# A tuned attention and two-layer MLP kernel: another order of work in the first chunks, and late tiles laid out later

## The chip, the core and the metric

The kernel runs on one core of one Trainium2 chip. The metric is the device time in microseconds of one execution. A core has a matrix engine (TensorE, PE), three engines for elementwise work (VectorE or DVE, ScalarE or ACT, GpSimd or POOL), and a queue engine (SyncE, SP) that issues most of the transfers here. Each engine works through its own list of instructions in order; semaphores between the lists hold an instruction back until what it needs is done.

## The reference

Three parts follow one another. First a gated linear attention over 4 batches, 8 heads, 768 positions, head dimension 48; then a SiLU layer; then a gated SiLU layer.

```python
for t in range(S):                                   # S = 768
    state = alpha[:, :, t, :, None] * state + einsum('bhd,bhe->bhde', k[:, :, t], v[:, :, t])
    y[:, :, t] = einsum('bhd,bhde->bhe', q[:, :, t], state)
x = y as (3072, 384)
h = x @ w_in;  x1 = silu(h) @ w_out                  # d_ff = 2048
out = (silu(x1 @ w_gate) * (x1 @ w_val)) @ w_out2    # d_ff = 1536
```

## The kernel before, in words

The attention is cut into chunks of 128 positions: 6 per batch, 24 in all, numbered so that chunk n belongs to batch n % 4. In a chunk the 8 heads lie in 4 pairs, and a "duo" d is two pairs, so chunk n has duos 2n and 2n + 1. For a chunk, VectorE makes two running products of alpha (scan_r with a reciprocal, scan_g); GpSimd multiplies keys and queries by them (kq, two instructions per chunk, line 443); TensorE makes the scores of each duo (scores2, 16 small matmuls, line 463); VectorE applies the causal mask and writes pt (mask2, line 474); ScalarE copies the scaled keys out (keys2, line 480); TensorE multiplies by the values and adds up the state (pv, lines 654 to 677); ScalarE and VectorE split the result into a high and a low part (chunk_high, chunk_end) as input x of the first layer, since the products are done in two float32r parts.

The first 7 chunks (NF = 7, blocks 0 and 1 of the token blocks) are done ahead of everything else by early(m), called for m = 0 to 6. early(m) makes the scores of chunk m and the products pv of chunk m - 1, and it prepares chunk m + 2 (scans and kq). In chunks 0 to 3 (NE = 4) the values of the first pair are also spread into a second tile v3 by GpSimd (spread, line 686). filler issues matmuls of the mask with itself into the part of the yd tile that nobody reads; they are called clock keepers in the change. The yd tile holds the results of pv; from m = 3 on it also serves, before pv writes it, as scratch space for decoding one unit of the first layer's weights (early_unit: three VectorE passes, lines 93, 98 and 103, and later a high and a low part). The loop over the 7 chunks is the whole opening of the kernel; after it the first layer runs turn by turn (g1, act1, g2 over steps), with the later chunks of attention and the remaining weight decoding threaded in, and then the second layer.

The order of work is written out by hand: each call above appends to the engines' lists, so the order of calls in early is the order in each engine's list. What SP issues is in such a list too: load_in(n) loads alpha, keys and queries of chunk n into one of two buffers and is called at the end of scan_g(n - 2); load_v(n) loads the values of chunk n, also into one of two buffers, and is called at the end of chunk_end(n - 2); load1 loads raw weight units, two per chunk. Of pt there are three buffers, each for one duo; of the score banks two, of the yd banks two.

open_late (line 346) lays out the tiles that the later chunks of attention use: GpSimd sets four of them to zero (line 351, 359) and ScalarE copies four identities (line 353). It stands between the opening and the first product's SiLU (act1, lines 840 and 841, with a VectorE subtract for the low part gl).

Of the kernel before, what the change touches and what calls it, by code (L numbers as in the profile page):

```python
# [23 lines left out]
NCH = B * NC  # L24
NP = H // 2
# [243 lines left out]
def fast(ctx, tc, pk, w1, w2, out, bad_i):  # L269
# [5 lines left out]
    blocks1, n = [], 0  # L275
# [91 lines left out]
    in_t, raw_in, v_t, r_t = {}, {}, {}, {}  # L367
# [35 lines left out]
            load_in(later_in.pop(0)[1])  # L403

    def load_v(n):
        if n >= NCH:
            return
        v_t[n] = ap.tile([128, NP, C], F32, tag="in_v", name=f"in_v{n}")
        SP.dma_start(
            out=v_t[n], in_=pk[n, :, A_W + 2 * W:].rearrange("p (r e) -> p r e", r=NP)  # L410
        )
# [6 lines left out]
    def scan_r(n, i, k):  # L418


        rg, cs = rg4[n % 2], slice(i * CA, (i + k) * CA)
        DVE.tensor_tensor_scan(
            out=rg[:, 0, cs][:, ::-1], data0=in_t[n][0][:, cs.start + 1:cs.stop + 1][:, ::-1],
            data1=ones4[:, i:i + k].rearrange("p i t -> p (i t)")[:, ::-1], initial=0.0,
            op0=ALU.mult, op1=ALU.add,
        )
        DVE.reciprocal(
            out=rc4[:, i:i + k, 0], in_=rg[:, 0].rearrange("p (i t) -> p i t", i=NP)[:, i:i + k, 0]
        )

    def scan_g(n, i, k):


        rg, cs = rg4[n % 2], slice(i * CA, (i + k) * CA)
        DVE.tensor_tensor_scan(
            out=rg[:, 1, cs], data0=in_t[n][0][:, cs],
            data1=rc4[:, i:i + k].rearrange("p i t -> p (i t)"), initial=0.0, op0=ALU.mult, op1=ALU.add,
        )
        by_pair = rg.rearrange("p x (i t) -> p x i t", i=NP)
        for lo in range(i, i + k, 2):  # L440
            d = (n * NP + lo) // 2
            kq_t[d] = kqs[d % 6]
            (DVE if d == 0 else POOL).tensor_tensor(
                out=kq_t[d][:, :, :2 * C].rearrange("p i (x t) -> p x i t", x=2),
                in0=in_t[n][1][:, :, lo:lo + 2], in1=by_pair[:, :, lo:lo + 2, 1:], op=ALU.mult,
            )
        c, b = divmod(n, B)
        if c:
            for p in range(i, i + k):
                t = state[b][:, p]  # L450
                ACT.activation(out=t, in_=t, func=AF.Copy, scale=by_pair[:, 0, p, 0:1])
        if i + k == NP:
            load_in(n + 2)
# [15 lines left out]
    def mask2(d, s):  # L469

        pt = ap.tile([128, 2, 2, C], F32, tag="pt", name=f"pt{d}", bufs=3)
        pt_t[2 * d], pt_t[2 * d + 1] = pt[:, 0], pt[:, 1]
        wide = mask.rearrange("p (a o t) -> p a o t", a=1, o=1).to_broadcast([128, 2, 2, C])
        DVE.tensor_tensor(out=pt, in0=s[:, :, :, :C], in1=wide, op=ALU.mult)
# [7 lines left out]
    def early(m):  # L482

        if m == 0:
            yd_place(0)
        s = {}
        for d in (2 * m, 2 * m + 1):
            filler(max(m - 1, 0), 4 if d == 1 else 1)  # L490
            s[d] = scores2(d)
        if m:
            pv(m - 1)
        for d in s:
            mask2(d, s[d])
            keys2(d, s[d])
            if m == 0:
                (scan_r if d == 0 else scan_g)(1, 0, NP)
        if m:
            chunk_high(m - 1)  # L500
            yd_place(m)
        if m < NE:
            spread(m)
        if m + 2 < NF:
            scan_r(m + 2, 0, NP)
            scan_g(m + 2, 0, NP)
        if m >= 3:
            early_unit(yd_t[m][:, 512:])
        if m:
            chunk_end(m - 1)  # L510
        up_to("gd", 2 * m, guard, ND)
        up_to("l1", 2 * m + 1, load1, NU1)
# [91 lines left out]
    def yd_place(n):  # L604

        t = yd_t[n] = banks((6, 2)[(NF - 1 - n) % 2] if n < NF else 6, f"yd{n}")
        y_t[n] = t[:, 256:768]

    def filler(n, times):

        wide = mask.rearrange("p (o t) -> p o t", o=1).to_broadcast([128, 4, C])
        for _ in range(times):
            PE.matmul(
                yd_t[n][:, :512].rearrange("p (o t) -> p o t", o=4), mask, wide, start=True, stop=True
            )
# [22 lines left out]
    def pv(n):  # L638

        c, b = divmod(n, B)
        v = v_t[n]
        if n >= NF:
            yd_place(n)
        y = y_t[n]
        first, last = n * NP, n * NP + NP
        heads = [(p, h, slice(64 * h, 64 * h + 64)) for p in range(NP) for h in range(2)]
        pts = [pt_t.pop(g) for g in range(first, last)]
        for p, h, hs in heads:  # L650
            if n < NE and p == 0:
                continue
            cs, r = slice(p * C, p * C + C), half(p, h)
            PE.matmul(  # L654
                y[r:r + 64, cs], v[:, p, hs], pts[p][:, h], start=p in (n < NE, 2), stop=True,
                skip_group_check=True,
            )
            if n < NE:
                PE.matmul(
                    y[r:r + 64, cs], v3[n % 2][:, p - 1, hs], pts[0][:, h], start=False, stop=True,  # L660
                    skip_group_check=True,
                )
        if c < NC - 1:
            ds = ds_t[n] = yd_t[n][:, 768:768 + NP * D].rearrange("p (r e) -> p r e", r=NP)
            for p, h, hs in heads:
                PE.matmul(
                    ds[hs, p], kt_t[first + p][:, hs], v[:, p, 64 * h:64 * h + D],
                    start=False, stop=True, skip_group_check=True,
                )
            for g in range(first, last):  # L670
                kt_t.pop(g)
        if c:
            for p, h, hs in (heads[2 * p + h] for p in (0, 2, 1, 3) for h in range(2)):
                r = half(p, h)
                PE.matmul(
                    y[r:r + D, p * C:p * C + C], state[b][hs, p],
                    kq_t[(first + p) // 2][(hs, p % 2, slice(C, 2 * C)) if n < NF else (hs, 1, p % 2)],
                    start=False, stop=True,
                    skip_group_check=True,
                )  # L680

    def spread(n):


        t = v3[n % 2].rearrange("p k (h x) -> p k h x", h=2)
        POOL.tensor_copy(
            t[:, :, :, D:],
            v_t[n][:, 0].rearrange("p (h x) -> p h x", h=2)[:, :, :D].rearrange(
                "p h (k r) -> p k h r", k=KT
            ),  # L690
        )

    def chunk_high(n):

        c, b = divmod(n, B)
        y = y_t[n].rearrange("p (r t) -> p r t", r=NP)
        j, i = chunk_blk[n]
        if i == 0:
            x_t[j] = big(block_place(j), f"x{j}", F32R).rearrange("p (x k t) -> p x k t", x=2, k=KT)
            if j:  # L700
                y3_t[j] = mp.tile([128, 2, 512], F32R, tag="y3", name=f"y3_{j}", bufs=1)
        cs = slice(i * C, i * C + C)
        if urgent(n):
            return
        ACT.activation(
            out=x_t[j][:, 0, :, cs], in_=y[:, 1:], func=AF.Copy, accum_out=ysum[:, 0, n:n + 1]
        )
# [127 lines left out]
    def act1(j, f):  # L835
        w = len(blocks1[j]) * C
        hb = h_t.pop((j, f))
        gh = mp.tile([128, 512], F32R, tag="gh", name=f"gh{j}_{f}")[:, :w]
        gl = mp.tile([128, 512], F32R, tag="gl", name=f"gl{j}_{f}")[:, :w]
        ACT.activation(out=gh, in_=hb, func=AF.Silu)  # L840
        ACT.activation(out=hb, in_=hb, func=AF.Silu)  # L841
        act_t[j, f] = (gh, gl)

        def rest():
            sub(DVE, gl, hb, gh)

        return rest
# [701 lines left out]
    attn(1, False)  # L1549
    up_to("gd", first_d - 1, guard, ND)  # L1550
    estack.close()
    open_late()
    g1(0)
    rest = act1(*steps[0])
    units1()
    rest()
    for s, (j, f) in enumerate(steps):
        need1(2 * f + 1)
        if s == 0:
            units1()  # L1560
        n = 19 + 2 * (s + 3 - len(steps))
        if s + 1 < len(steps):
            need1(2 * steps[s + 1][1])
            if n >= 19:
                run(OUTPUT[n] - PAIR)
            g1(s + 1)
        slot(s, 0, (lambda: act1(*steps[s + 1])) if s + 1 < len(steps) else None)
        if n >= 19:
            if s + 1 < len(steps):
                free_banks.append((s + 1) % 2)  # L1570
            run(OUTPUT[min(n + 1, 23)] - PAIR)
        g2(j, f)
        slot(s, 1)

    wstack.close()
    free_banks += [2, 3, 4]
# [90 lines left out]
```

## Time and profile before

| | |
|---|---|
| time, median of 3 runs | 947.0 us (943.33 to 947.2) |
| profiled execution | 947.71 us, span 946.0 us |
| TensorE busy | 905.8 us (96%) |
| VectorE busy | 611.6 us (65%) |
| ScalarE busy | 451.4 us (48%) |
| GpSimd busy | 279.4 us (30%) |
| mean granted clock of TensorE | 0.982 of full speed |
| moved by DMA | 150.89 MB, mean 160 GB/s |

The span runs from the first to the last instruction that the profiler records; the time of the execution is a little longer. Busy shares are means over stages that have different limits, so they don't say by themselves what bounds a stage. Idle time of an engine is put down to what released it. The granted clock is the share of TensorE's full speed that it was given.

### The profile page before, as it was taken

How to read it: one execution, taken by the hardware profiler on the slowest of the kernel's cores; microseconds unless marked ns; L12 is line 12 of the kernel's file. 1: busy time of each engine (PE TensorE's matmuls, PEld its weight loads, DVE VectorE, ACT ScalarE, POOL GpSimd, SP SyncE). 2: the span in 40 equal slices, each digit the busy share in tenths (PEclk: the TensorE clock that was granted, in tenths of full speed). 3: DMA queues.
4: the chain of work that ended last, by engine and by line, in shares of the span. 5: the costliest groups of instructions: out<-in, count | busy, mean ns of one | idle time of the engine just before them, and what ended most of it. 6: DMA issues, size and time to landing. Idle time of an engine off the chain costs nothing.

```text
span 946.0 us, 14403 instructions
## 1 busy us (share of the span) xinstructions
PE 905.8 (96%) x5261; PEld 771.9 (82%) x5261; DVE 611.6 (65%) x1079; ACT 451.4 (48%) x1005; POOL 279.4 (30%) x389
## 2 busy tenths in 40 slices
PE   7569999999999999999999999999999999999996
PEld 4458998889999998888888888878888878888785
DVE  7569966556767577466258457786467875577732
ACT  1355544555556465455446444453454444444432
POOL 5311004528868789677318200000000000000000
PEclk8789999999999999999999999999999999999998
DMA  6665301233564465542466466632557513855301
GB/s 214 203 216 200 118 1 66 84 124 116 181 205 143 155 198 169 177 131 103 134 220 226 173 234 224 242 117 84 201 211 284 188 34 118 283 180 220 134 1 70
DMA packets 43007, 150.89 MB, mean 160 GB/s; under 512 B 4400, under 2 KB 9008, under 8 KB 40240
## 3 DMA queue, kind: packets, MB, share of 16 engines
q1 hardware_dynamic: 42304, 149.30, 46.3%
q8 instruction: 43, 0.70, 0.3%
q10 hardware_dynamic: 624, 0.59, 0.2%
q14 instruction: 36, 0.29, 0.1%
HBM read 118.03 MB, written 29.88 MB: 156 GB/s over the span
## 4 chain that ended last, share of the span: by engine, by line
PE 86%; DVE 3%; issue 3%; DMA 2%; POOL 2%; ACT 2%; SPq 1%; ACTq 0%; POOLq 0%
PE o L1257 15%; PE h L823 6%; PE x L872 6%; PE x L873 6%; PE x L875 6%; PE h L824 6%; PE h L826 6%; PE D L1194 5%; PE A L1194 5%; PE E L1194 5%; PE yd L654 3%; PE K L1194 2%; PE B L1194 2%; PE G L1194 2%; PE H L1194 2%
## 5 line engine op out<-in xcount | busy, mean ns | idle before, releaser
L322 DVE TENSOR_TENSOR gl<-h,gh 128x384 fp32r<-128x384 f32 (+1 forms) x112 | 68.5, 612 | 90.9 <-ACT h L841 85.6
L872 PE MATMUL x<-gh,w 128*128 128x384 f32 (+1 forms) x336 | 121.2, 361 | 4.3 <-DVE x1e L881 2.2
L823 PE MATMUL h<-x,w 128*128 128x384 f32 (+1 forms) x336 | 122.6, 365 | 1.8 <-DMA x<-y 1.6
L873 PE MATMUL x<-gh,w 128*128 128x384 f32 (+1 forms) x336 | 120.8, 360 | 0.0
L824 PE MATMUL h<-x,w 128*128 128x384 f32 (+1 forms) x336 | 120.8, 359 | 0.0
L840 ACT ACTIVATE gh<-h 128x384 fp32r<-128x384 f32 (+1 forms) x112 | 59.9, 535 | 101.1 <-PE h L826 99.7
L1257 PE MATMUL o<-gh,ring 128*128 128x512 f32 x288 | 88.7, 389 | 0.0
L875 PE MATMUL x<-gl,w 128*128 128x384 f32 (+1 forms) x336 | 84.5, 359 | 0.0
L826 PE MATMUL h<-x,w 128*128 128x384 f32 (+1 forms) x336 | 84.3, 358 | 0.0
L872 PEld LDWEIGHTS x<-gh,w 128*128 128x128 f32 x336 | 63.1, 188 | 10.6 <-DVE x1e L881 2.7
L823 PEld LDWEIGHTS h<-x,w 128*128 128x128 f32 x336 | 63.1, 188 | 10.6 <-issue 5.4
L531 POOL TENSOR_TENSOR kq<-in,r 128x256 f32<-128x256 f32 x34 | 33.7, 990 | 118.6 <-DVE r L520 118.6
L873 PEld LDWEIGHTS x<-gh,w 128*128 128x128 f32 x336 | 63.1, 188 | 5.2
L824 PEld LDWEIGHTS h<-x,w 128*128 128x128 f32 x336 | 63.1, 188 | 5.0
L875 PEld LDWEIGHTS x<-gl,w 128*128 128x128 f32 x336 | 61.4, 188 | 6.0 <-DVE gl L322 0.2
L826 PEld LDWEIGHTS h<-x,w 128*128 128x128 f32 x336 | 61.4, 188 | 5.9
L1257 PEld LDWEIGHTS o<-gh,ring 128*128 128x128 f32 x288 | 54.1, 188 | 11.2
L841 ACT ACTIVATE h<-h 128x384 f32<-128x384 f32 (+1 forms) x112 | 59.6, 533 | 0.0
L1257 PE MATMUL o<-gl,ring 128*128 128x512 f32 x144 | 56.4, 392 | 0.8 <-DVE gl L322 0.8
L322 DVE TENSOR_TENSOR gl<-a,gh 128x512 fp32r<-128x512 f32 x48 | 32.8, 691 | 37.3 <-ACT gh L1246 36.2
L1194 PE MATMUL A<-mov,ring 128*128 128x512 f32 x198 | 55.6, 389 | 0.0
L1194 PE MATMUL D<-mov,ring 128*128 128x512 f32 x198 | 55.6, 389 | 0.0
(219 smaller groups left out, 1951.8 us busy)
## 6 DMA issues: line engine op xcount, KB each, us to landing
ring<-comb_d SPq DMA_DIRECT2D x21, 1920.0 KB, 7.7
raw<-in_w_dram SPq DMA_DIRECT2D x58, 384.0 KB, 4.4
in<-in_pk_dram SPq DMA_DIRECT2D x22, 770.5 KB, 4.4
ring<-wo_d SPq DMA_DIRECT2D x6, 1920.0 KB, 7.4
comb_d<-area SPq DMA_DIRECT2D x8, 896.0 KB, 4.9
in_v<-in_pk_dram SPq DMA_DIRECT2D x24, 256.0 KB, 3.9
comb_d<-area SPq DMA_DIRECT2D x8, 640.0 KB, 5.1
x1r<-x_d SPq DMA_DIRECT2D x6, 768.0 KB, 8.9
```

What stands on the lines that cost most here:

```text
L322: eng.tensor_tensor(out=lo, in0=src, in1=hi.bitcast(F32), op=ALU.subtract)
L531: POOL.tensor_tensor(out=kq_t[d][:, 0], in0=in_t[n][1][:, 0, ps_], in1=r_t[d][:, :, 1:], op=ALU.mult)
L823: PE.matmul(acc, part(u, k), xh, start=(k == 0), stop=False)
L824: PE.matmul(acc, part(u, k, 1), xh, start=False, stop=False)
L826: PE.matmul(acc, part(u, k), xl, start=False, stop=(k == len(xk) - 1))
L840: ACT.activation(out=gh, in_=hb, func=AF.Silu)
L841: ACT.activation(out=hb, in_=hb, func=AF.Silu)
L872: PE.matmul(x1_t[j][m], part(u, m), gh, start=(f == 0), stop=False)
L873: PE.matmul(x1_t[j][m], part(u, m, 1), gh, start=False, stop=False)
L875: PE.matmul(x1_t[j][m], part(u, m), gl, start=False, stop=(f == NF1 - 1))
L1194: PE.matmul(acc, s(hs, r), x[:, hx], start=op in new and i == 0, stop=i == 2, skip_group_check=True,)
L1257: PE.matmul(o_t[b][m], part(ring_t[p, f], m, l), x, start=(f == 0 and i == 0), stop=(f == NF2 - 1 and i == 2),)
```

## The change

In early(m): spread comes at the top, ahead of the scores. From chunk 1 on the two keepers come no longer one ahead of each duo's scores, but both behind pv(m - 1), and into the yd tile of chunk m. load_v(m + 1) is issued right behind pv(m - 1); load_v skips a chunk that is already loaded. The scans of chunk m + 2 come between the masks of the chunk's two duos, and chunk_high(m - 1) ahead of the second mask. In chunk 0 the scores, keepers and scans keep their order.

After the opening, open_late is called no longer ahead of the first step but behind the step with number 2, and the first act1 with its VectorE part is put ahead of the next weight units.

```diff
     def load_v(n):
-        if n >= NCH:
+        if n >= NCH or n in v_t:
             return
...
+        if m < NE:
+            spread(m)
         if m == 0:
             yd_place(0)
         s = {}
         for d in (2 * m, 2 * m + 1):
-            filler(max(m - 1, 0), 4 if d == 1 else 1)
+            if m == 0:
+                filler(0, 4 if d else 1)
             s[d] = scores2(d)
         if m:
             pv(m - 1)
+            load_v(m + 1)
+            yd_place(m)
+            filler(m, 2)
+
         for d in s:
+            if m and d % 2:
+                chunk_high(m - 1)
             mask2(d, s[d])
             keys2(d, s[d])
-            if m == 0:
-                (scan_r if d == 0 else scan_g)(1, 0, NP)
-        if m:
-            chunk_high(m - 1)
-            yd_place(m)
-        if m < NE:
-            spread(m)
-        if m + 2 < NF:
-            scan_r(m + 2, 0, NP)
-            scan_g(m + 2, 0, NP)
+            if d % 2 == 0:
+                if m == 0:
+                    scan_r(1, 0, NP)
+                elif m + 2 < NF:
+                    scan_r(m + 2, 0, NP)
+                    scan_g(m + 2, 0, NP)
+        if m == 0:
+            scan_g(1, 0, NP)
+            scan_r(2, 0, NP)
+            scan_g(2, 0, NP)
         if m >= 3:
             early_unit(yd_t[m][:, 512:])
...
     estack.close()
-    open_late()
     g1(0)
-    rest = act1(*steps[0])
+    act1(*steps[0])()
     units1()
-    rest()
...
         g2(j, f)
         slot(s, 1)
+        if s == 2:
+            open_late()
```

## Rows read from the trace of the kernel before

**Rows 1.** Stretches: busy time of each engine, granted clock, DMA share, GB/s.

```profile
0.00:73.45 73.45, 48.73 (x576) 32.27 (x576) 47.79 (x78) 27.86 (x92) 24.46 (x41) 0.81 0.64 208
73.45:140.00 66.55, 66.55 (x345) 61.70 (x346) 58.55 (x129) 32.32 (x68) 0.14 (x2) 1.00 0.32 108
```

**Rows 2.** Timeline, first products of chunks 1, 2, 3, 4 and 6 with the values.

```profile
21.62 0.43 PE L654 MATMUL yd<-pt,in_v 128*64 128x128 f32 x2
...
31.79 0.90 PE L654 MATMUL yd<-pt,in_v 128*64 128x128 f32 x3 [1.32 <-DMA in_v<-in_pk_dram]
...
44.02 0.70 PE L654 MATMUL yd<-pt,in_v 128*64 128x128 f32 x4
...
55.26 1.34 PE L654 MATMUL yd<-pt,in_v 128*64 128x128 f32 x16
...
64.93 1.09 PE L654 MATMUL yd<-pt,in_v 128*64 128x128 f32 x16 [1.49 <-issue]
```

**Rows 3.** Waits from 0 to 75 us: total, times, longest.

```profile
DVE pt L474 <- PE yd L654: 12.0, 4, 5.6
POOL start L686 <- DMA in_v<-in_pk_dram: 12.0, 2, 6.0
...
PE yd L613 <- DVE raw L103: 10.7, 3, 4.7
```

**Rows 4.** Timeline of SP, three value loads.

```profile
26.26 0.42 SPq L409 DMA_DIRECT2D in_v<-in_pk_dram  x1
...
34.84 0.43 SPq L409 DMA_DIRECT2D in_v<-in_pk_dram  x1
...
43.36 0.37 SPq L409 DMA_DIRECT2D in_v<-in_pk_dram  x1
```

**Rows 5.** Landing of the tile of alpha, keys and queries, 0 to 75 us.

```profile
DMA to landing us min/median/max: 3.1/4.3/6.3
```

**Rows 6.** VectorE from 13.5 to 70 us, groups by form: busy, mean ns.

```profile
L474 DVE TENSOR_TENSOR pt<-s,mask 128x512 f32<-128x512 f32 x12 | 8.1, 686 | 15.6 <-PE yd L654 12.0 <-PE s L463 3.4 <-PE yd L659 0.2
...
L435 DVE TENSOR_TENSOR_SCAN rg<-in,rc 128x516 f32<-128x516 f32 x5 | 6.2, 1233 | 0.2
L322 DVE TENSOR_TENSOR x<-yd,x 128x384 fp32r<-128x384 f32 x6 | 3.3, 544 | 0.0
L98 DVE SCALAR_TENSOR_TENSOR yd<-raw,yd 128x384 int32<-128x384 int32 x4 | 2.2, 562 | 0.1
...
L322 DVE TENSOR_TENSOR y<-yd,y 128x128 fp32r<-128x128 f32 x3 | 0.9, 284 | 0.8 <-ACT y L730 0.8
L764 DVE TENSOR_TENSOR state<-yd,state 128x192 f32<-128x192 f32 x2 | 0.7, 358 | 0.9 <-ACT y L758 0.9
```

**Rows 7.** Timeline, products kq of chunk 2 and a scan that meets them.

```profile
18.41 2.32 POOL L443 TENSOR_TENSOR kq<-in,rg 128x512 f32<-128x512 f32 x2 [3.63 <-DVE rg L435]
...
19.68 2.14 DVE L422 TENSOR_TENSOR_SCAN rg<-in,ones 128x516 f32<-128x516 f32 x1
```

**Rows 8.** Timeline of TensorE: a keeper, scores, end of pv(1), scores behind a pause.

```profile
19.46 0.39 PE L613 MATMUL yd<-mask 128*128 128x512 bf16 x1
...
19.78 0.83 PE L463 MATMUL s<-kq 64*64 64x176 f32 x16
...
23.30 0.67 PE L666 MATMUL yd<-in_v,kt 128*64 128x48 f32 x16
...
40.71 1.45 PE L463 MATMUL s<-kq 64*64 64x176 f32 x16
```

**Rows 9.** Timeline around the first SiLU.

```profile
71.97 0.80 ACT L353 ACTIVATE qh<-start 128x96 fp32r<-128x96 f32 x4 [1.42 <-POOL qh L351]
...
73.45 0.50 PE L872 MATMUL x<-gh,w 128*128 128x512 f32 x1 [2.07 <-ACT gh L840]
```

**Rows 10.** Timeline, one gl on VectorE and its first use on TensorE.

```profile
115.73 0.55 DVE L322 TENSOR_TENSOR gl<-h,gh 128x384 fp32r<-128x384 f32 x1
...
116.95 0.68 PE L875 MATMUL x<-gl,w 128*128 128x384 f32 x3
```

## The prediction

> **What bounds the kernel now.** I read the stretches first. From 73.45 us on TensorE is busy without a hole: 66.55 of 66.55 us up to 140 [rows 1], and behind that the same work goes on to the end. Before 73.45 it is busy 48.73 us, VectorE 47.79 and GpSimd 24.46, at a granted clock of 0.81, a mixture of the full level, 2.4 GHz, and the half one, 1.2 GHz [rows 1]. So nothing but the opening can give time, and what it gives shifts all the rest to the left. The change touches the opening alone, and its first late step.
>
> I call p(n) the moment at which the products of chunk n with the values start on TensorE (pv, line 654). They stand at p(1) 21.62, p(2) 31.79, p(3) 44.02, p(4) 55.26 and p(6) 64.93 [rows 2]: ten to twelve microseconds for a chunk in the middle, where pv itself needs 2.35 at full clock (from 21.62 to the end of its state products at 23.97) [rows 2, 8].
>
> The view of waits says what fills a chunk. There are two circles.
>
> *The values' circle.* GpSimd's copy of the values (spread, line 686) waits 12.0 us in two times for the transfer in_v [rows 3]. That transfer is issued on SP behind load_in, which waits for GpSimd's products kq, which stand behind spread. The value loads therefore come at 26.26, 34.84 and 43.36, 8.55 us apart [rows 4]: transfer, copy, products, next transfer.
>
> *The mask circle.* The second mask of a chunk needs a pt buffer that pv of the chunk before frees, and VectorE waits 12.0 us in four times there [rows 3]; the scans and the weight decode are queued behind it. At the next chunk the clock keeper (filler) writes the tile that the decode uses, and TensorE waits 10.7 us in three times for the last pass, with the scores queued behind the keeper [rows 3]. So products, mask, scans, decode, keeper and scores stand one behind the other: 11.24 us from p(3) to p(4) [rows 2].
>
> **The change, part by part.** I work out the new p(n) from durations of the profiled execution: a mask 0.69, a scan 1.23 where nothing disturbs it, a decode pass 0.56 (three to a unit, 1.75 with handovers), the subtract of x 0.55, the state's add 0.36, the subtract of y 0.28 [rows 6]; a group of scores 0.83 at full clock and 1.45 at half, a keeper 0.39 [rows 8]; both products kq of a chunk 2.32 [rows 7]. Two scans with the reciprocal take 2.65.
>
> *Value copy first.* On GpSimd the order changes only in chunk 0, where the copy goes ahead of the products of chunk 1; GpSimd has nothing else to do there until scan_g(1) is done. Cost nothing; if the values came late, it would push these products by the lateness.
>
> *Value load behind pv(m-1).* One load is moved on SP ahead of load_in(m+4). It waits for pv(m-1), and load_in behind it waits for kq(m+2), which ends later in the schedule below. The circle now goes over two chunks: 8.55 becomes 4.3 per chunk, no longer a bound. The number of transfers stays, and is discussed with the rivals.
>
> *Scans between the masks.* This costs where pv came early anyhow. In chunk 1 the scan of chunk 3 meets kq(2), which ends at 20.73, and took 2.14 [rows 7]; it can't end sooner than that allows, so scan_g(3) ends at 23.3, then mask 0.69, a copy by ScalarE of some 0.35 (estimate), and the second scores, which before had their mask done in time. TensorE has been idle, so they take 1.45: p(1) is 25.8 in place of 21.62, 4.2 lost. If the scan slips between the two kq it is 24.7; if VectorE is held twice, 27. I take the value nearest to the row.
>
> From there: pv(1) at half clock, some 3.5 (estimate, 2.35 at full and 4.7 at double), two keepers 0.9, two scores 1.66: p(2) 31.9 against 31.79. The long wait for the values is gone, but the loss has eaten it.
>
> p(3): pv(2) 2.35, two keepers 0.8, then the decode 1.75 (the keeper now writes its tile first): 36.8. On VectorE the mask of the first half starts at 31.05, scans to 34.4, second mask to 35.1: ready in time. The scans' input is issued behind kq(3), at 23.3 + 2.32 and a handover, near 25.7, and lands 4.3 later [rows 5], before 31.05. Gain 7.2.
>
> p(4): VectorE bounds. Subtract 0.55, mask 0.69, scans 2.65, mask 0.69, decode 1.75 make 6.33: 43.2 with the handovers, gain 12.1. The scores no longer stand behind the decode, so they run under it.
>
> p(5) and p(6): no scans. From p(4), pv 2.1 (estimate, a little under 2.35, since it has no spread values but the state's products), keepers 0.8, decode 1.75 make 4.7. Then VectorE: subtract 0.55, state and y 0.64, a wait for ScalarE's y of some 0.5 (estimate), two masks 1.38, a subtract of weights 0.55, decode 1.75, in all 5.3. p(6) is 53.2 against 64.93: **11.7 us gained**. After p(6) the two orders are the same until the late tiles.
>
> *Keepers behind pv.* Two to a chunk as before. If they no longer hold the clock, TensorE pays, see below. They also wait for the bank of chunk m-2, whose last reader is done one chunk earlier: nothing.
>
> *Late tiles after step 2.* ScalarE's four copies wait 1.42 for GpSimd's memset, take 0.80, and only then comes the first Silu; TensorE waits 2.07 for it [rows 9]. Without them it starts up to 2.05 sooner. But VectorE is the second bound here: 58.55 us busy in the stretch to 140 [rows 1], and late in it gl is ready at 116.28 when line 875 uses it at 116.95: 0.67 of slack [rows 10]. VectorE gains only some 0.5 itself, because it now waits for the Silu before it goes on decoding. TensorE's other 1.55, less the slack of 0.67, come back as waits of some 0.9. I book **1.1** (bounds 0.5 and 2.05). The moved copies and memsets cost nothing where they go: ScalarE is busy 32.32 of 66.55 us [rows 1]. Were that cover gone, 0.80.
>
> The sum: 11.7 + 1.1 = 12.8. The profiled execution took 947.71 (span 946.0, 1.7 around it), so 934.9; the median shown, 947.0, is 0.7 below it, well within the 0.5% (4.7 us) that a measurement of this kernel can tell from no change.
>
> **A rule against it.** The scans now run closer to GpSimd's products. A scan that met them took 2.14 in place of 1.23 [rows 6, 7], 0.91 more. The Trainium skill (SBUF — State Buffer, "SBUF: two separate sides") says that VectorE with two SBUF inputs and a GpSimd operation that reads SBUF lock a port pair for a whole instruction, and the other fully blocks. The trace agrees: 2.14 beside 1.23. By that rule the sum would be that of the third rival below, if all scans met a product.
>
> **The rivals.**
>
> 1. *The clock stays at the half level* (chance 0.12). For it: the opening is at 0.81 [rows 1], and behind a pause such as chunk 1 now has the scores took 1.45 [rows 8]. Against: from p(2) on the pauses shrink. Price: pv and keepers of chunks 3 and 4 take some 1.8 more each, chunks 5 and 6 some 1.5 together: 5.1, so 940.0.
>
> 2. *Chunk 1's pace stays* (0.06). If the mask behind the scans holds every chunk up as it does chunk 1, each needs some 9 us: p(4) is 25.8 + 3 x 9 = 52.8, p(6) 62.8, gain 2.1 + 1.1: 944.5, no change that can be told. It speaks for it that VectorE's order is now fixed mask, scan, scan, mask; against it that kq is by then a chunk ahead.
>
> 3. *All scans meet GpSimd's products* (0.10). Four more scans, of chunks 5 and 6, at 0.91: 3.6, so 938.5.
>
> 4. *Slower: the masks now stand behind transfers* (0.05). The second mask, and pv with it, waits for scans, and these for `in`. kq(2) ends at 20.73; then twice a landing L, with scans and products (5.0) between, and mask and decode after the second scans: p(4) is about 31 + 2L, and p(6) ten later. Level with before at L near 12.5 us; the landings seen are 3.1 to 6.3 [rows 5]. The opening moved 208 GB/s [rows 1] and must now move the same in 53.2 in place of 64.93, about a fifth more per time. With L = 16 p(6) is 73 and the run 954.7. It decides only if the queue doubles its longest landing.
>
> The forecast as summed has 0.67.
>
> **Numbers.** Likeliest 934.9. Its own bounds: p(1) at 24.7 and the whole 2.05 give 932.8 and, with masks that come in time for p(5) and p(6), 931; held twice and 0.5 for the late tiles give 937. Rivals 1 and 3 reach to 940, with a little of both 942. Range 930.5 to 942: it leaves out rivals 2 and 4 and some odds, less than 2 in 10. Faster: forecast, rivals 1 and 3, 0.89; same 0.06; slower 0.05.
>
> **What would show it.** SP issues the value load of chunk 2 near 21 and not 26; the waits of spread for in_v, of the second mask for pv, and of the keeper for the decode are gone or small. p(1) is later than 21.62, p(2) about equal, p(4) twelve sooner. The first line 872 starts 13 to 14 sooner than 73.45, and some line 875 now waits for gl. Wrong: p(4) later than 48, `in` landing over 8, scans of 2 us in chunks 5 and 6, or a clock under 0.8 behind p(2).

## The result and the profile after

The changed kernel takes 936.83 us in the median of 6 executions (935.0 to 939.12), the kernel before 947.1 beside it (943.33 to 949.05). The ratio is 0.9898, 95% interval 0.9874 to 0.9922: 1.0% faster, 9.7 us by the ratio and 10.3 by the medians. Forecast were 934.9 and a gain of 12.8. The profiled execution has a span of 936.9 us against 946.0.

In the stretches of the profile after (columns as in [rows 1]) the opening, up to the first product with gh, is 60.43 us long, 13.0 shorter than in [rows 1], at a granted clock of 0.86 and 249 GB/s. Behind it TensorE is no longer busy without a hole.

```profile
0.00:60.43 60.43, 44.84 (x576) 32.29 (x576) 44.24 (x74) 27.18 (x88) 23.47 (x38) 0.86 0.74 249
60.43:126.00 65.57, 65.32 (x329) 58.10 (x328) 59.86 (x131) 31.89 (x71) 1.92 (x5) 1.00 0.34 114
```

The timeline after, first products of chunks 1, 2, 3, 4 and 6, to be set beside [rows 2] (line 663 is line 654 of before):

```profile
24.90 0.50 PE L663 MATMUL yd<-pt,in_v 128*64 128x128 f32 x4
...
30.33 0.45 PE L663 MATMUL yd<-pt,in_v 128*64 128x128 f32 x4
...
35.54 0.45 PE L663 MATMUL yd<-pt,in_v 128*64 128x128 f32 x4 [0.37 <-DVE raw L103]
...
41.84 1.65 PE L663 MATMUL yd<-pt,in_v 128*64 128x128 f32 x16 [0.37 <-DVE raw L103]
...
52.72 1.97 PE L663 MATMUL yd<-pt,in_v 128*64 128x128 f32 x16 [2.10 <-DVE raw L103]
```

p(1) is 3.3 us later than before and p(2) 1.5 sooner; then the lead is 8.5 at p(3), 13.4 at p(4) and 12.2 at p(6). What TensorE waits for ahead of pv is now the decode itself, and of [rows 3] none of the three waits is left. The waits after, from 13 to 58 us (total, times, longest), have that wait in two groups, and one of the scores for the keys' copy, whose longest is chunk 2's scores behind the late second mask of chunk 1:

```profile
PE s L463 <- ACT kt L480: 6.1, 3, 3.7
PEld yd L663 <- DVE raw L103: 4.9, 4, 2.6
...
PE yd L663 <- DVE raw L103: 3.4, 4, 2.1
```

SP after, the loads of chunks 2, 3 and 4: that of chunk 2 is issued at 20.44 in place of 26.26. Chunk 3's still comes 8.0 us later, because it stands behind the late pv(1); from then on the loads are 4.0 and 5.2 us apart (the next at 37.63), not 8.55 [rows 4].

```profile
20.44 0.42 SPq L409 DMA_DIRECT2D in_v<-in_pk_dram  x1
...
28.46 0.33 SPq L409 DMA_DIRECT2D in_v<-in_pk_dram  x1
...
32.42 0.62 SPq L409 DMA_DIRECT2D in_v<-in_pk_dram  x1
```

**The lead at the end of the decoding.** I compare the same instruction in both timelines. At the first product with gh the lead is 73.45 - 60.43 = 13.0 us. At the last gl that stands in the stretch of weight decoding it is 11.0, for VectorE (126.26 - 115.25) and for TensorE (126.86 - 115.86). Before, two rows of VectorE and one of TensorE:

```profile
70.58 0.36 DVE L744 TENSOR_TENSOR state<-yd,state 128x192 f32<-128x192 f32 x1
...
126.26 0.55 DVE L322 TENSOR_TENSOR gl<-h,gh 128x384 fp32r<-128x384 f32 x1
...
126.86 0.79 PE L875 MATMUL x<-gl,w 128*128 128x384 f32 x3
```

and after, the same three:

```profile
59.54 0.36 DVE L753 TENSOR_TENSOR state<-yd,state 128x192 f32<-128x192 f32 x1
...
115.25 0.56 DVE L322 TENSOR_TENSOR gl<-h,gh 128x384 fp32r<-128x384 f32 x1
...
115.86 0.79 PE L884 MATMUL x<-gl,w 128*128 128x384 f32 x3
```

VectorE leaves the opening 11.04 us sooner and reaches that gl 11.01 sooner: the late tiles gave it nothing. TensorE, which ran 13.0 ahead, has come back to VectorE's lead.

**Where two more went.** From the end of block 1 (VectorE's copy x1e, 156.44 before, 145.44 after) to that of block 0 (203.44 and 194.31) the lead falls from 11.0 to 9.1. In between the first product of block 2 waits for its rows in both executions, 1.63 before and 1.66 after. In the new one a second wait of 0.63 follows, and the clock is at the half level for a while: a matmul of 512 columns takes 0.63 in place of 0.40. TensorE after:

```profile
187.56 0.41 PE L832 MATMUL h<-x,w 128*128 128x384 f32 x1 [1.66 <-DMA x<-y]
187.81 0.34 PE L833 MATMUL h<-x,w 128*128 128x384 f32 x1
188.78 0.47 PE L832 MATMUL h<-x,w 128*128 128x384 f32 x1 [0.63 <-DMA x<-y]
...
191.40 0.63 PE L882 MATMUL x<-gh,w 128*128 128x512 f32 x1
```

### The profile page after: what moved, and what is told of

It is laid out like the page before. It is cut to its first block, busy times and chain, and to the rows that moved or that the text cites. A ratio compares the mean times of both kernels' runs of the same rounds, so it can differ in the third digit from the quotient of the medians.

```text
span 936.9 us, 14400 instructions
## 1 busy us (share of the span) xinstructions
PE 905.0 (97%) x5261; PEld 772.8 (82%) x5261; DVE 610.7 (65%) x1079; ACT 450.7 (48%) x1005; POOL 279.8 (30%) x389
## 4 chain that ended last, share of the span: by engine, by line
PE 79%; DVE 7%; issue 3%; DMA 2%; ACT 1%; POOL 1%; SPq 1%; POOLq 0%; ACTq 0%; DVEq 0%
PE o L1266 15%; PE h L832 5%; PE x L881 5%; PE x L882 5%; PE x L884 5%; PE D L1203 5%; PE A L1203 5%; PE h L835 5%; PE h L833 5%; PE E L1203 5%; PE yd L663 2%; PE K L1203 2%; PE B L1203 2%; PE G L1203 2%; PE F L1203 2%
## 5 line engine op out<-in xcount | busy, mean ns | idle before, releaser
L1266 PEld LDWEIGHTS o<-gh,ring 128*128 128x128 f32 x288 | 54.1, 188 | 11.2
```

What stands on the lines that cost most here:

```text
L1266: PE.matmul(o_t[b][m], part(ring_t[p, f], m, l), x, start=(f == 0 and i == 0), stop=(f == NF2 - 1 and i == 2),)
```

## The experiments

All were timed beside the kernel before, 6 or 12 executions each. Executions of one and the same kernel differ by 4 us and more (935.0 to 939.12 for the changed kernel, 942.9 to 951.9 for the one before over all these series), so the timelines tell more than the medians; the ratio of each run is to the kernel before of its own series. The marks, in us, are from each run's profiled execution: p(n); the first product h of line 823 (832); the first product with gh, line 872 (881); the end of block 1, taken at the VectorE copy x1e; and the stretch from h to that end.

| run | p(2) | p(4) | p(6) | h | gh | block 1 | h to block 1 | ratio (95%) |
|---|---|---|---|---|---|---|---|---|
| before | 31.79 | 55.26 | 64.93 | 66.99 | 73.45 | 156.44 | 89.45 | 1 |
| whole change | 30.33 | 41.84 | 52.72 | 56.22 | 60.43 | 145.44 | 89.22 | 0.9898 (0.9874-0.9922) |
| e1 opening only | 31.40 | 42.56 | 51.91 | 53.97 | 60.45 | 144.89 | 90.92 | 0.9902 (0.9877-0.9928) |
| e2 late tiles only | 31.03 | 53.47 | 63.29 | 65.35 | 69.58 | 154.85 | 89.50 | 0.9998 (0.998-1.0016) |
| e3 values only | 28.66 | 49.28 | 58.72 | 60.78 | 67.23 | 150.22 | 89.44 | 0.9967 (0.995-0.9984) |
| e4 scans only | 30.60 | 46.99 | 56.42 | 58.48 | 64.93 | 147.95 | 89.47 | 0.9909 (0.9885-0.9934) |
| e12 keepers only | 30.89 | 48.14 | 62.44 | 65.59 | 71.78 | 154.78 | 89.19 | 0.9973 (0.9952-0.9995) |
| e5 keepers ahead | 30.25 | 45.79 | 55.21 | 57.27 | 61.51 | 146.80 | 89.53 | 0.9924 (0.9895-0.9953) |
| e6 chunk 1's masks first | 31.07 | 43.09 | 52.44 | 54.50 | 58.78 | 144.05 | 89.55 | 0.9909 (0.9874-0.9944) |
| e7 keepers ahead of pv(6) | 31.28 | 42.36 | 51.71 | 53.77 | 58.05 | 143.31 | 89.54 | 0.9913 (0.9882-0.9943) |
| e8 two decode passes | 30.09 | 42.34 | 53.09 | 55.15 | 59.43 | 142.33 | 87.18 | 0.9877 (0.9847-0.9907) |
| e9 low parts on GpSimd | 31.65 | 42.73 | 52.49 | 54.55 | 58.78 | 148.83 | 94.28 | 0.9909 (0.988-0.9938) |
| e10 keepers at block 2 | 31.62 | 42.69 | 52.03 | 54.09 | 58.37 | 143.60 | 89.51 | 0.9910 (0.9879-0.9942) |
| e11 e9 and e10 together | 30.46 | 42.61 | 53.48 | 56.91 | 61.12 | 151.18 | 94.27 | 0.9950 (0.993-0.9969) |

The opening of e2 is that of before, instruction for instruction, and its p(6) is 1.6 us sooner: a mark of the opening is good to about that.

**The two halves of the change.** e1 keeps the old late tiles, e2 the old opening.

```diff
 e1, against the changed kernel
+    open_late()
     g1(0)
-    act1(*steps[0])()
+    rest = act1(*steps[0])
     units1()
+    rest()
...
-        if s == 2:
-            open_late()
```

> Only the reordered opening, with the late tiles laid out ahead of the first step as before. Theory (VectorE takes the late tiles' gain back): the first line 872 product starts about 10.8 us sooner than before (62.7), later than with the whole change (60.4), and yet TensorE never waits for gl afterwards, so that 10.8 is still there at the end: a time within 1 us of the whole change, about 936 to 937. Rival (the late tiles give their 2.2 us for good): 938.5 to 939.5.

Ratio 0.9902, median 936.0, beside 0.9898 and 936.83 of the whole change: as far as the times can tell, the opening alone gives the whole gain. The marks expected were not met, though. Its pv(6) ran at full clock, so h came at 53.97, and gh at 60.45. TensorE waited 2.09 for the Silu and then ran at half clock, which costs it 1.5 us more up to block 1 (90.92).

```profile
60.45 0.80 PE L881 MATMUL x<-gh,w 128*128 128x512 f32 x1 [2.09 <-ACT gh L849]
61.05 0.63 PE L882 MATMUL x<-gh,w 128*128 128x512 f32 x1
```

e2 has the opposite halves:

```diff
 e2, against the kernel before
-    open_late()
     g1(0)
-    rest = act1(*steps[0])
+    act1(*steps[0])()
     units1()
-    rest()
...
+        if s == 2:
+            open_late()
```

> Only the late tiles laid out behind step 2, with the opening as before. Theory (VectorE takes it back): the first product with gh starts about 2.2 us sooner, at 71.2, but its lead over the kernel before has shrunk to under 0.5 us by the time the weight decoding ends (near 130 us): time within 0.1% of before. Rival: the lead stays at 2 us, ratio near 0.998.

From h to gh it takes 4.23 us in place of 6.46, so the 2.2 us are there; from h to block 1's end it takes 89.50 in place of 89.45, so they are gone again. The ratio of 0.9998 agrees, but its interval (0.998 to 1.0016, some 1.7 us either way) could not by itself tell nothing from the 1.1 us of the prediction.

**Is it VectorE that takes them back?** e8 takes work away from VectorE and nothing else. It leaves out the third decode pass (the three lowest bits of a weight's mantissa) of the units decoded behind the opening.

```diff
 e8, in decode_unit
+            if step == 2 and key[0] == "1" and key not in in_bank:
+                raw_t[key] = raw_t[key].bitcast(F32).rearrange("p (n two) -> p n two", two=2)[:, :, 1]
+                return
```

> The whole change, but units of the first layer's weights that are decoded behind the opening leave out the third VectorE pass (the three lowest bits of the mantissa). This takes 0.55 us of VectorE's 2.0 per unit away. Theory (VectorE is what takes back 13.15 - 11.0 us between 61 and 126 us): no product waits for gl, the lead of 13 us over before holds to 126 us, and the run is 2 us faster than the whole change (about 934.5 to 935). Rival (TensorE's own clock or the transfers take it back): unchanged.

The stretch shrinks to 87.18, 2.3 us shorter than the 89.5 of every kernel with all passes whose stretch nothing else disturbed: the 2.2 us of the late tiles. From gh on it needs 82.90, what the kernel before needs from there (82.99), whose gh comes 2.2 us later behind h. Waits of the weight loads for gl, whole change and then e8 (the last columns are the idle time before the group and its releaser):

```profile
L884 PEld LDWEIGHTS x<-gl,w 128*128 128x128 f32 x60 | 10.5, 188 | 2.3 <-DVE gl L322 1.1
```

```profile
L887 PEld LDWEIGHTS x<-gl,w 128*128 128x128 f32 x60 | 10.9, 188 | 0.9
```

That is 1.4 us. Another 1.2 stand at gh: the loads of line 881 sit idle for 2.4 us in the whole change (1.5 of it waiting for ScalarE's gh) and those of the same line in e8 for 1.2. This is VectorE's decode too, one engine further on: ScalarE's copy w of a decoded unit stands ahead of gh in its list, and from 60 to 126 us it waits 25.0 us in 21 times for the third pass. The ratio is 0.9877 (0.9847 to 0.9907) and can't be told from the whole change's 0.9898. VectorE's part is shown by the marks.

e9 tried to use this: idle GpSimd makes the low part of every fourth unit.

```diff
-        up_to("s1", st["h1"] - 1, lambda u: low_unit(("1", u), DVE), NU1)
+        up_to("s1", st["h1"] - 1, lambda u: low_unit(("1", u), POOL if u % 4 == 2 and u > 4 else DVE), NU1)
```

> The whole change, with the low part of every fourth weight unit decoded behind the opening (7 of 28) subtracted by GpSimd, which is idle there, in place of VectorE: 7 x 0.55 = 3.9 us less for VectorE. Theory (VectorE takes the late tiles' gain back): from the first product of line 832 to the end of block 1 it takes 87.2 us as with two passes, not 89.5; the run is up to 2 us faster than the whole change, less than the 4 us by which executions of one kernel differ. Rival (GpSimd reading SBUF holds VectorE up as long as it relieves it): 89 us or more, no gain.

The stretch grew to 94.28. The rival was right. The largest part is one collision. GpSimd's first subtract pushed the late tiles' memsets back, and a decode pass of VectorE (line 93, 0.36 us elsewhere) that met them took 3.72; gl came late, TensorE waited 3.32 and went on at half clock. GpSimd, VectorE and TensorE of e9:

```profile
66.24 1.15 POOL L322 TENSOR_TENSOR w<-raw,w 128x384 fp32r<-128x384 f32 x1 [23.23 <-ACT w L813]
67.34 1.27 POOL L351 MEMSET qh<- 128x1408 f32 x1
68.55 0.94 POOL L351 MEMSET ql<- 128x1024 f32 x1
...
69.95 0.10 POOL L360 MEMSET ones<- 128x2 f32 x1
```

```profile
66.55 3.72 DVE L93 TENSOR_SCALAR dec<-raw 128x384 int32<-128x384 int32 x1
...
71.25 1.30 PE L884 MATMUL x<-gl,w 128*128 128x384 f32 x3 [3.32 <-DVE gl L322]
```

Without that collision the move would not have helped either. Each of the other six subtracts met one instruction of VectorE and made it 0.7 to 0.8 us longer (0.55 to 1.36 or 1.39 four times, 0.36 to 1.07 twice), more than the 0.55 that it took off VectorE. One of the six:

```profile
86.42 1.16 POOL L322 TENSOR_TENSOR w<-raw,w 128x384 fp32r<-128x384 f32 x1 [7.95 <-ACT w L813]
86.60 1.39 DVE L98 SCALAR_TENSOR_TENSOR raw<-raw,dec 128x384 int32<-128x384 int32 x1
```

**The parts of the opening.** Each move alone:

```diff
 e3, against the kernel before
-        if n >= NCH:
+        if n >= NCH or n in v_t:
...
         if m:
             pv(m - 1)
+            load_v(m + 1)
```

> Only the value load behind pv, the rest of the opening and the late tiles as before. Theory (two circles, the mask circle is as long as the values' one): p(2) comes some 1.3 us sooner because the values are there, but the circle of products, mask, scans, decode, keeper and scores stays at 11 us a chunk: 1 to 2 us gained at p(6), ratio 0.998 to 0.999. Rival (the values' circle was the bound): 5 to 7 us, ratio 0.993 to 0.995.

My expectation was wrong in size and the rival nearer: p(6) 6.2 us sooner, ratio 0.9967. Half of it is at p(2), 3.1 sooner (28.66) and not 1.3. From there to p(4) a chunk takes 10.3 us (11.7 before, 11.2 in e2 with the same opening): the mask circle stood, a little shorter.

```diff
 e4, against the kernel before
             keys2(d, s[d])
             if m == 0:
                 (scan_r if d == 0 else scan_g)(1, 0, NP)
+            elif d % 2 == 0 and m + 2 < NF:
+                scan_r(m + 2, 0, NP)
+                scan_g(m + 2, 0, NP)
...
-        if m + 2 < NF:
-            scan_r(m + 2, 0, NP)
-            scan_g(m + 2, 0, NP)
+        if m == 0:
+            scan_r(2, 0, NP)
+            scan_g(2, 0, NP)
```

> Only the scans between a chunk's masks; value loads, keepers, late tiles as before. Theory: p(1) is lost by 3 us (24.9) without effect on p(2), which waits for values near 31.8; then the mask circle without the scans is 8.5 us, as long as the values' circle, so p(3) is near 40.4 and p(4) near 49; p(6) near 59, 6 us gained, ratio 0.993 to 0.995. Rival (the scans' place hardly matters, the values decide): p(3) stays near 44, ratio above 0.998.

p(6) is 8.5 us sooner and the ratio 0.9909, more than expected and within the interval of the whole change. With kq earlier, SP gets to the value loads earlier too, although their place in its list is the old one. SP of e4:

```profile
25.00 0.42 SPq L409 DMA_DIRECT2D in_v<-in_pk_dram  x1
...
30.36 0.43 SPq L409 DMA_DIRECT2D in_v<-in_pk_dram  x1
...
35.71 0.37 SPq L409 DMA_DIRECT2D in_v<-in_pk_dram  x1
```

They are 5.4 us apart, not 8.55. The scans' place thus opens the mask circle and most of the values' circle.

```diff
 e12, against the kernel before
-            filler(max(m - 1, 0), 4 if d == 1 else 1)
+            if m == 0:
+                filler(0, 4 if d else 1)
             s[d] = scores2(d)
         if m:
             pv(m - 1)
+            yd_place(m)
+            filler(m, 2)
...
-            yd_place(m)
```

> Only the keepers behind pv, in the new chunk's tile; values, scans and late tiles as before. Theory (any one of the three moves breaks a part of the same circle, as the runs with values alone and scans alone showed 6.2 and 8.5 us at p(6)): the scores no longer wait for the decode, 5 to 8 us at p(6), ratio 0.992 to 0.995. Rival (keepers matter only together with the scans, because the second mask still holds scans and decode back): under 3 us.

p(4) came 7.1 us sooner but p(6) 2.5, ratio 0.9973. The lead falls to 4.9 at p(5), which stands at 56.43: the values of chunk 5 are issued at 51.15 only, behind loads 8.6 us apart, and TensorE waits 2.8 us for them. Behind this wait pv(5) ran at half clock (3.56 us from its first product to the keepers, 2.06 at full clock), and the second mask and the decode queue behind it; that takes the rest. The values' circle is whole and takes the keepers' gain back. Alone the three moves give 6.2 + 8.5 + 2.5 = 17.2 us at p(6), together some 12: they cut the same loops.

e5 undoes the keepers' place in the whole change:

```diff
             if m == 0:
-                filler(0, 4 if d else 1)
+            filler(max(m - 1, 0), 4 if d == 1 else 1)
...
-            filler(m, 2)
```

> The whole change, but the two keepers of a chunk ahead of its scores again, in the tile of the chunk before. Theory (the decode, the keeper and the scores then stand one behind the other again): from chunk 4 on each chunk needs the scores' 1.7 to 3 us more, at half clock where TensorE pauses; p(6) 6 to 9 us later than 52.7, time 942 to 946. Rival (the keepers' place only matters for the clock): under 2 us later.

p(6) is 55.21, 2.5 us later than in the whole change and later than in all versions with its keepers (51.71 to 53.48); the ratio is 0.9924, its interval overlaps with that of the whole change. The rival (under 2 us) was nearer than the theory: the keeper that waits for the decode costs some 2.5 us once the other two moves are made, less than my lower bound of 6.

e6 puts the scans of chunk 3 behind both masks of chunk 1, since nothing there needs them so early:

```diff
-                elif m + 2 < NF:
+                elif 1 < m < NF - 2:
...
+        if m == 1:
+            scan_r(3, 0, NP)
+            scan_g(3, 0, NP)
```

> The whole change, but in chunk 1 both masks go ahead of the scans of chunk 3. Theory (chunk 1's loss is hidden at p(2) by ScalarE, whose guards wait for kq(3)): p(1) is back near 21.6, p(2) at 29.5 to 30, and p(6) no more than 0.5 us sooner: no difference that can be timed. Rival (the 3.3 us lost in chunk 1 are on the path): p(2) near 27, p(6) near 49.5, 3 us faster than the whole change.

p(1) is 20.55, and p(2) 31.07, no sooner than the whole change's 30.33: chunk 1's loss is not on the path. p(6) is 52.44 and the median 937.21, no difference.

e7 adds six keepers (keep issues the same matmuls as filler) while TensorE waits ahead of pv(6):

```diff
+    keep(pools_ps["early"].tile([128, 2, 512], F32, tag="s0", name="keep")[:, 0], 6)
     st["qk"], st["pv"] = first, NF - 1
```

> The whole change, with six more keepers in a free score bank while TensorE waits for the decode ahead of the last pv. Theory: pv(6) runs at full clock again (2.1 us in place of 3.6), the first line 881 product comes some 1.4 us sooner, and VectorE, which bounds the next stretch, takes most of it back: 0 to 1 us faster than the whole change. Rival: the keepers hold pv(6) up, 1 us slower.

From p(6) to h it takes 2.06 us, in the whole change 3.50. But e1, e5, e6, e8, e9 and e10 need 2.06 without these keepers, while e11 needs 3.43 and e12 3.15: a slow pv(6) comes in some executions and not in others. Ratio 0.9913, nothing gained: inconclusive.

**The clock behind block 2's wait.** e10 lets TensorE work while it waits for the rows of block 2; e11 adds e9's edit.

```diff
 e10, in g1
-        h_t[j, f] = bank(s % 2, f"h{j}_{f}")[:, :w]
+        hb = bank(s % 2, f"h{j}_{f}")
+        if j == 2 and f == 0:
+            keep(hb, 6)
+        h_t[j, f] = hb[:, :w]
```

> The whole change, with six clock keepers written into the bank of the first product of block 2, which waits 1.7 us for the rows x from y. Theory (what is lost behind 126 us is the clock, which falls behind that wait in some executions): no stretch below full clock between 180 and 200 us, block 1's end to block 2's end 47.1 us and not 48.9, and the slowest executions 1.5 to 2 us sooner. Rival (the wait itself is the loss): 48.9 stays or the keepers delay the product by another microsecond.

In the timeline it looks like what was expected (the stretch that the expectation names ends in fact at block 0's end): 190.91 - 143.60 = 47.3 us against 48.9 in the whole change, 47.0 in before, and 50.4 in e8. TensorE's wait shrinks to 0.33. But e1, e5 and e9 have 47.3 as well, without these keepers and with the wait whole, so it is not shown that they held the clock. A stretch around the product in e10 and then in the whole change, with the granted clock before the DMA share:

```profile
186.00:191.00 5.00, 4.41 (x22) 3.73 (x21) 0.65 (x2) 1.60 (x4) 0.00 (x0) 1.00 0.21 61
```

```profile
187.50:192.50 5.00, 4.30 (x13) 3.75 (x14) 0.39 (x1) 0.87 (x2) 0.00 (x0) 0.66 0.24 65
```

The median is 937.14 and the slowest execution 941.31, so nothing shows in the times. The clock fell in e10's profile at 350 to 360 us instead (0.83 over these 10 us).

> The whole change with both: low parts of every fourth unit on GpSimd, and keepers ahead of block 2's first product. Theory: the two effects add, 3 to 4 us faster than the whole change, near 933. Rival (the later stretches, where the clock also falls in some executions, level it out): within 1 us of the whole change.

Ratio 0.9950 against 0.9898, some 5 us slower than the whole change. e9's collision is in it (94.27, the pass of line 93 takes 3.71), which its theory had not foreseen. In the profiles 2.4 us of its lag behind e9 stand at h already (56.91 against 54.55: pv(6) ran at half clock); the rest stays open. No version that I ran is shown to beat the changed kernel.

## Why the prediction was right, point by point

- *Only the opening can give time.* Right for this pair of executions: behind block 0 the lead no longer changes beyond 1 us (9.1 us there, 9.1 in the spans). In a single execution of another version it can: in e6 it is 10.5 at block 0 and 12.5 in the spans, although nothing there was changed.
- *The new p(n).* Forecast 25.8, 31.9, 36.8, 43.2, 53.2; measured 24.90, 30.33, 35.54, 41.84, 52.72. The loss in chunk 1 is there and, as e6 shows, harmless. Of the path between, the decode ahead of pv is what TensorE waits for from p(3) to p(6), as summed. The lead was larger at p(4) than forecast (13.4 against 12.1) and fell to 12.2 at p(6), because pv(4) ran at half clock here: its 16 products take 1.65 us, those of pv(5) 1.09.
- *The opening's term.* 11.7 booked, 12.2 measured at p(6). In this execution pv(6) then ran at half clock and gave 1.4 back (h 10.8 sooner), in others not. The cause by parts was told less well than the sum: I took the two circles for separate, each with its own cure. e4 shows that kq ties them together, and that the scans' place alone gives most.
- *The late tiles' term.* This is the step that was mis-sized: "I book 1.1". The start was right, 2.2 us sooner against 2.05. But VectorE's own gain, put at 0.5, is 0.0 (11.04 and 11.01), and the slack of 0.67 in [rows 10] is not the smallest: ten microseconds later, at 126.26 + 0.55 against 126.86, it is 0.05. So all comes back and the term is zero: 89.50 against 89.45 in e2. e8 shows that it is VectorE that takes it. The time still met the forecast because this term was only 1.1 of 12.8.
- *The rivals.* The scans that meet GpSimd's products: of the five first scans (line 422) of chunks 2 to 6 one did (2.08; 1.23 to 1.28 for the others), and before it was two (2.14 and 2.00), so closer together they met less often. `in` landed in 6.8 at most, and VectorE's masks waited 0.2 us in all. The half clock in the opening, rival 1, came in parts only, 0.86 for 0.81. Chunk 1's pace did not stay.
- *The 1.9 us behind.* Not in the prediction. Some 0.3 of it belongs to the new order: e1, e5 and e9 need 47.3 where before needs 47.0, with the clock full in all four and a second wait of 0.6 that before does not have. The rest is the clock, which fell behind a wait that was there before too. It falls there in e2, with the opening of before, and not in e1, with the new one, so it is not the change alone; whether the second wait makes it more frequent stays open (the half level follows in four of the seven profiles that have it, and in one of the five in which it is 0.2 at most).

The sum for the profiled execution: 12.2 at p(6), less 1.4 for pv(6), plus 2.2 for the late tiles, makes 13.0; less 2.0 to VectorE, less 1.9 at block 2, nearly all of it the clock: 9.1, the difference of the spans.

## What to carry to other kernels

When a start is moved forward, ask which engine is the second bound of the stretch behind it, and look for its smallest slack over the whole stretch, not for one row: TensorE showed no hole there, and VectorE took all of 2.2 us back. Waits in an in-order queue tie circles together. Putting the work that feeds others (scans) ahead of a wait (the second mask) freed a transfer two queues further on (VectorE to GpSimd to SP), so single moves don't add up.

Where executions differ by more than the effect, compare marks of the same instruction in the timelines, and look at more than one execution for the clock.

## What the runs showed of the hardware

- A VectorE tensor_scalar pass of 0.36 us took 3.72 (3.71 in e11) when it met a GpSimd subtract and the memsets behind it: it ended at 70.27, behind the last of them (70.05). Before, the same pass took 1.13 beside one of these memsets and ended at 73.04, ahead of the last two (73.24 and 73.49), so it is not held up by all of them each time.
- A GpSimd subtract of two SBUF tiles (1.03 to 1.16 us) made the VectorE instruction that met it 0.7 to 0.8 us longer, in six of six cases in e9.
- A wait of TensorE of 1.6 to 1.7 us is followed by the half clock in some executions (whole change, e2, e6, e7, e8: 0.59 to 0.70 over the next 5 us) and not in others (before, e1, e3, e4, e5, e9, e12), at the same place of the program. It cost from 1.4 to 3.4 us between block 1's and block 0's end (46.9 to 47.4 without it; 48.4 in e2, 50.4 in e8).
